# Letting the last group's three table stores leave together, with a GpSimd drain behind each unit's gathers

## The chip, the cores and the metric

The kernel runs on one core of one Trainium2 chip. The metric is the device time of one execution in microseconds (us). A core has five engines that run side by side: TensorE (PE, with its weight loads as PEld), VectorE (DVE), ScalarE (ACT), GpSimd (POOL) and SyncE (SP). SP issues most transfers; POOL issues those whose rows are picked by an index tile. One transfer is carried by the core's DMA engines and reports its end through a semaphore.

## The reference

Three stages follow one another: a pooled attention, a dense two-layer block, and a mixture of experts in which each token goes to the one expert with the largest logit.

```python
x = attention(q, k, v)                       # 2304 tokens of 512
h = x @ w_in; g = where(h >= 1, h, where(h <= -1, 0, (h + 1)**2 / 4)); x = g @ w_out
logits = normalise(x) @ normalise(expert_emb).T / tau
e = argmax(logits); gate = softmax(logits)[e]
out[token] = gate * (relu(x[token] @ w1[e]) @ w2[e])      # 8 experts, d_ff 1024
```

## The kernel before, in words

Attention runs over pairs of heads, the dense block over four groups of token tiles (five, five, five and three tiles of 128 tokens). The rows of each finished group are written to `y_rows` in DRAM, and the `Router` works out, per group, each token's expert, its gate, and its place in a table in DRAM (`self.tab`). An entry of the table is four words: the row of `y_rows`, the row of the output, the gate, and nothing. Each expert has its own stretch of the table. The entries of one tile are written by one indirect store that POOL issues (`scatter`, L924 to L927): index column `i` of `pu` says where the 128 entries of tile `i` go. For the first three groups these stores are put into a list and issued later, two per step; for the last group they follow at once, in a loop (L928 to L932).

The expert stage (`Moe2`) goes through units of 256 table entries of one expert. For unit `u`, `gather` (L1180) lets SP read the first table row of the unit from the small tile `units` (L1181), load the unit's 256 entries (`records`, L1186) into a tile `d_rec`, and lets POOL fetch the token rows these entries name by two indirect gathers (`rows`, L1191) into tiles `d_xg`. TensorE transposes them (`x_t`, `x_tile`, L1198), ACT and DVE split them into a high and a low part (L1202, L1203), and `hidden` (L1219) and `outer` (L1255) are the two layers. POOL stores the results by output row (`store`, L1263). All engines run the order in which the code is written; POOL's order is therefore: the last group's three table stores, the two gathers of unit 1, the store of unit 0's first half, the store of its second half, the gathers of unit 2, and from then on for each unit its stores and then the gathers of the unit after next. A unit with at most 128 tokens takes the shorter `half` path (L1224) and has one store.

Unit 0 is special. Its expert is known early, from the first three groups, and its work (`hidden` and `outer` in `run`, L1337 to L1367) runs while the last group is still being routed. Unit 1 is the first that needs the table complete. Between the end of the last group's logits and unit 1 the chain is: DVE computes `pu` (L922), POOL issues the three stores one by one, each behind the landing of the one before, because all three write the tile `self.tab`; DVE meanwhile works out the units (`units`, L1026, its result at L1072); SP reads `units` and loads `d_rec`; POOL gathers; TensorE transposes. On SP the loads of unit 1's weights stand behind the load of `d_rec`; the weights are the same as unit 0's here, so that these loads are skipped by their condition.

The tiles `d_rec` are a ring of three, `d_xg` and `d_ob` (outputs and the shorter path's intermediates) rings of four, so an engine that falls behind holds up the others only when a ring is used up.

Of the kernel before, what the change touches and what calls it, by code (L numbers as in the profile page):

```python
# [8 lines left out]
F32 = mybir.dt.float32  # L9
# [18 lines left out]
UNIT = 256  # L28
# [662 lines left out]
class Router:  # L691
# [9 lines left out]
    def consts(self, stage):  # L701
        nc, t, g = self.nc, self.one.tile, self.nc.gpsimd
        kw = dict(allow_small_or_imprecise_dtypes=True)
        self.iota = t([128, E], F32, name="iota_e")
        g.iota(self.iota, pattern=[[1, E]], base=-E, channel_multiplier=0, **kw)
        self.base = t([128, E], F32, name="base_e")
        g.iota(self.base, pattern=[[N, E]], base=0, channel_multiplier=0, **kw)
        self.iu = t([1, UMAX + 1], F32, name="iota_u")
        g.iota(self.iu, pattern=[[1, UMAX + 1]], base=0, channel_multiplier=0, **kw)
        yield  # L710
        self.two = t([1, UMAX + 1], F32, name="powers")
        g.memset(self.two[:, 0:1], 1.0)
        a = 1
        while a <= UMAX:
            m = min(a, UMAX + 1 - a)
            g.tensor_scalar(out=self.two[:, a:a + m], in0=self.two[:, 0:m], scalar1=2.0 ** a, scalar2=1.0,
                            op0=ALU.mult, op1=ALU.mult)
            a += m
        yield
        self.acc = t([128, E], BF16, name="acc")  # L720
        g.memset(self.acc, 0.0)

        self.ids = t([128, 18, 4], U32, name="ids")
        g.memset(self.ids.bitcast(F32), 0.0)
        ids = self.ids.bitcast(I32)
        g.iota(ids[:, 0:15, 0], pattern=[[128, 15]], base=0, channel_multiplier=1)
        g.iota(ids[:, 15:18, 0], pattern=[[128, 3]], base=ZROW + 1, channel_multiplier=1)
        yield
        for p0, n, tile0 in ((0, 4, 0), (4, 1, 16), (5, 12, 4), (17, 1, 17)):
            if n > 1:  # L730
                g.iota(ids[:, p0:p0 + n, 1], pattern=[[NQ, n // 4], [128, 4]], base=tile0 // 4 * NQ,
                       channel_multiplier=1)
                continue
            for h in range(2):
                p = slice(h * 64, h * 64 + 64)
                g.iota(ids[p, p0:p0 + 1, 1], pattern=[[0, 1]], base=(2 * (tile0 - 16) + h) * NQ + 512,
                       channel_multiplier=1)
        yield

        n = E * N // 128  # L740
        rows = stage.tile([128, 1024], I32, name="m", tag="m")[:, 0:4 * n]
        for c, v in enumerate((ZROW, 4095, 0, 0)):
            g.iota(rows.rearrange("p (r c) -> p r c", c=4)[:, :, c], pattern=[[0, n]], base=v, channel_multiplier=0)
        nc.sync.dma_start(out=self.tab.rearrange("(p r) c -> p (r c)", p=128), in_=rows.bitcast(U32))
        nc.sync.dma_start(out=self.y[ZROW:ZROW + 1, :].rearrange("a (p c) -> (a p) c", p=8), in_=self.cn["zero"][0:8])
        yield
        ones, upper = (stage.tile([128, 512], F32, name="w", tag="w")[:, 0:128] for _ in range(2))
        g.memset(ones, 1.0)
        g.affine_select(out=upper, in_=ones, pattern=[[1, 128]], compare_op=ALU.is_gt, fill=0.0,
                        base=0, channel_multiplier=-1)  # L750
        self.ones = t([128, 128], BF16, name="ones_b")
        g.tensor_copy(self.ones, ones)
        self.upper = t([128, 128], BF16, name="upper_b")
        g.tensor_copy(self.upper, upper)
        self.tau = t([128, 1], F32, name="tau")
        nc.sync.dma_start(out=self.tau, in_=self.tau_in.to_broadcast([128, 1]))
# [34 lines left out]
    def group(self, g, yps, m1, m2):  # L791

        nc = self.nc
# [25 lines left out]
        def small(name, dt=F32):  # L819
            return sm.tile([128, 5, E], dt, name=name)[:, :nt]  # L820

        def one(name, dt=F32):
            return sm.tile([128, 5], dt, name=name)[:, :nt]
# [15 lines left out]
        def transpose(i):  # L839
            def f():  # L840
                if last and i < 2:
                    p = m2.pt()
                else:
                    p = (spare[i % 2] if spare else bank("yt_ps")).rearrange("p (k t) -> p k t", k=4)
                for k in range(4):
                    nc.tensor.transpose(p[:, k], ys[i][:, k * 128:(k + 1) * 128], self.cn["idf"])
                yt = d["yt", i] = yts()

                def ev():
                    if i % 2:  # L850
                        nc.vector.tensor_copy(yt, p)
                    else:
                        nc.scalar.copy(yt, p)
                    if not last:
                        square(i)
                return ev() if last else ev
            return f
# [53 lines left out]
        def ev():  # L911
            ids = self.ids[:, p0:p0 + nt]
            p = d["p"]
            r, pf, pu = small("rk"), one("pf"), one("pu", U32)
            nc.vector.tensor_tensor(out=r, in0=p[:, 0:nt * E].rearrange("p (t e) -> p t e", e=E),
                                    in1=self.base[:, None, :].to_broadcast(sh), op=ALU.add)
            nc.vector.tensor_reduce(out=d["s"], in_=d["ex"], axis=AX.X, op=ALU.add)
            nc.vector.tensor_tensor(out=r, in0=r, in1=d["oh"], op=ALU.mult)
            nc.vector.tensor_scalar_add(d["s"], d["s"], 1e-9)
            nc.vector.tensor_reduce(out=pf, in_=r, axis=AX.X, op=ALU.add)  # L920
            nc.vector.reciprocal(ids[:, :, 2].bitcast(F32), d["s"])
            nc.vector.tensor_copy(pu, pf)  # L922

            def scatter(i):  # L924
                nc.gpsimd.indirect_dma_start(
                    out=self.tab, out_offset=bass.IndirectOffsetOnAxis(ap=pu[:, i:i + 1], axis=0),
                    in_=ids[:, i, :], in_offset=None)  # L927
            for i in range(nt):  # L928
                if last:
                    scatter(i)  # L930
                else:
                    m1.scat.append(lambda i=i: scatter(i))  # L932
            if not last and not spare:
                for i in range(nt):
                    nc.vector.tensor_add(self.acc, self.acc, d["oh"][:, i])
# [39 lines left out]
        out = []  # L975
        if spare:
            def both(i):
                def f():
                    t = transpose(i + 1)() if i + 1 < nt else lambda: None
                    e = logits(i)()  # L980
                    return lambda: (t(), e())
                return f
            out = [transpose(nd)] + [both(i) for i in range(nd, nt)]
# [120 lines left out]
class Moe2:  # L1104
# [74 lines left out]

    def gather(self, u):  # L1180
        row = self.nc.sync.value_load(self.rt.u[0:1, u, 0:1], min_val=0, max_val=E * N - UNIT)  # L1181
        rec = self.records(row, self.rec())
        return rec, self.rows(rec, [self.xg() for _ in range(2)])

    def records(self, row, rec):
        self.nc.sync.dma_start(out=rec, in_=self.rt.tab[bass.ds(row, UNIT), :].rearrange("(t p) c -> p t c", p=128))  # L1186
        return rec

    def rows(self, rec, xs, n=N + 1):
# [315 lines left out]
```

## Time and profile before

| | |
|---|---|
| time, median of 3 runs | 1203.81 us (1201.74 to 1203.91) |
| the profiled execution's own time | 1205.57 us |
| its span, first to last instruction | 1203.8 us |
| mean granted TensorE clock | 0.983 of full speed |
| busy: PE, DVE, ACT, POOL | 1149.5, 883.3, 740.3, 600.7 us |

The span is what the rows below are counted in, from its start; 1.77 us of the profiled execution's time lie around it. The expert stage begins at about 917 us of the span, and from about 956 us unit 1 runs. A row of a timeline gives the start, the time taken, the engine, the line, what is written from what, the number of instructions, and in brackets the idle time of the engine before it and what ended it. Rows that are merged give the time from the first start to the last end.

### The profile page before, as it was taken

The page shows a single profiled execution, that of the slowest core. Times are in us where ns is not written, and L with a number is a line of the kernel's source. Part 1 is how long each engine was busy: PE and PEld are TensorE (multiplying, and loading weights), DVE is VectorE, ACT ScalarE, POOL GpSimd, SP SyncE. Part 2 cuts the span into 40 slices and gives each one's busy share as a digit, 9 for nine tenths or more (in the row PEclk, how much of TensorE's full clock was granted, in tenths as well). Part 3 has the DMA queues.
Part 4 walks back from the last instruction along what each step waited for, and adds up shares of the span by engine and source line. Part 5 has one row for each costly group of instructions (what it writes and reads, how often), then busy time and mean ns, then how long its engine had stood idle before and what let it go on. Part 6 is the DMA issues. An engine that isn't in the chain of part 4 may idle for free. (4 is left out here: it accounts for less than half of the span.)

```text
span 1203.8 us, 21165 instructions
## 1 busy us (share of the span) xinstructions
PE 1149.5 (95%) x7315; PEld 1068.2 (89%) x7315; DVE 883.3 (73%) x1593; ACT 740.3 (61%) x1451; POOL 600.7 (50%) x523
## 2 busy tenths in 40 slices
PE   7999999999999999799789999999999899999995
PEld 7999999999999999688679889988989798888794
DVE  6888988999999998698745664664444767576663
ACT  5888888878788787343335444444445466576663
POOL 7998988777888883699930230013020311122121
PEclk9999999999999999999899999999999899999998
DMA  7787777785868753564332212111240111376533
GB/s 187 179 184 179 165 186 171 171 209 126 205 162 205 173 137 103 158 194 147 101 106 65 66 45 76 56 34 31 97 159 27 40 51 38 116 256 191 177 106 110
DMA packets 87189, 156.14 MB, mean 130 GB/s; under 512 B 26871, under 2 KB 44279, under 8 KB 87056
## 3 DMA queue, kind: packets, MB, share of 16 engines
q1 hardware_dynamic: 82352, 142.34, 44.2%
q0 software_dynamic: 4336, 11.58, 2.9%
q8 instruction: 67, 1.10, 0.4%
q10 hardware_dynamic: 368, 0.59, 0.2%
q14 instruction: 66, 0.54, 0.2%
HBM read 145.84 MB, written 20.08 MB: 138 GB/s over the span
## 5 line engine op out<-in xcount | busy, mean ns | idle before, releaser
L235 DVE TENSOR_SCALAR_CACHE_REDUCE e<-sc 128x1152 f32<-128x1152 f32 x144 | 194.7, 1352 | 25.0 <-PE sc L231 23.8
L242 ACT ACTIVATE e<-e,nm 128x1152 f32<-128x1152 f32 x144 | 183.7, 1276 | 4.4 <-DVE e L235 4.4
L231 PE MATMUL sc<-kT,qt 128*128 128x384 f32 x780 | 159.8, 340 | 9.2 <-DVE e L235 7.5
L269 ACT CAST pth<-pa 128x768 fp32r<-128x768 f32 (+2 forms) x160 | 116.3, 737 | 83.4 <-PE pa L260 83.4
L271 DVE TENSOR_TENSOR ptl<-pa,pth 128x768 fp32r<-128x768 f32 (+2 forms) x160 | 138.8, 876 | 20.6 <-ACT pth L269 8.4
L1166 DVE TENSOR_TENSOR e<-e,e 128x512 fp32r<-128x512 f32 x200 | 129.4, 686 | 33.0 <-ACT e L1165 16.4
L582 DVE SCALAR_TENSOR_TENSOR u<-h,u 128x320 f32<-128x320 f32 (+1 forms) x112 | 55.7, 497 | 124.8 <-ACT u L581 124.7
L578 ACT ACTIVATE u<-h,half 128x320 f32<-128x320 f32 (+1 forms) x112 | 59.7, 533 | 139.1 <-PE h L563 125.6
L231 PEld LDWEIGHTS sc<-kT,qt 128*128 128x128 f32 x780 | 132.8, 189 | 11.5 <-DVE e L235 9.1
L1255 PE MATMUL d_po<-e,e 128*128 128x512 f32 x504 | 122.6, 396 | 0.5 <-DVE e L1166 0.5
L260 PE MATMUL pa<-idf,e 128*128 128x128 f32 x864 | 118.2, 273 | 1.7 <-DVE ptl L271 1.7
L1165 ACT CAST e<-e 128x512 fp32r<-128x512 f32 x200 | 113.7, 619 | 4.6 <-DMA e<-moe_w 4.1
L595 PE MATMUL y<-wh,gl 128*128 128x512 f32 x288 | 114.0, 396 | 0.5 <-POOL gl L586 0.5
L595 PE MATMUL y<-wh,gh 128*128 128x512 f32 x288 | 114.0, 396 | 0.0
L595 PE MATMUL y<-wl,gh 128*128 128x512 f32 x288 | 113.6, 395 | 0.0
L1263 POOL DMA_INDIRECT out<-d_ob,d_rec x19 | 21.9, 1154 | 181.1 <-ACT d_ob L1262 150.7
L1255 PEld LDWEIGHTS d_po<-e,e 128*128 128x128 f32 x504 | 93.5, 190 | 19.4 <-DVE e L1166 0.9
L260 PEld LDWEIGHTS pa<-idf,e 128*128 128x128 f32 x864 | 103.4, 141 | 7.1 <-DVE ptl L271 1.3
L584 ACT CAST gh<-u 128x320 fp32r<-128x320 f32 (+1 forms) x112 | 52.4, 468 | 87.3 <-DVE u L582 87.3
L563 PE MATMUL h<-xth,wh 128*128 128x320 f32 (+1 forms) x448 | 89.8, 322 | 16.6 <-POOL wh L57 9.8
L285 PE MATMUL av<-pth,vh 128*128 128x288 f32 x576 | 103.5, 307 | 0.0
L535 POOL TENSOR_TENSOR xl<-xth,xl 128x512 f32<-128x512 f32 (+1 forms) x14 | 18.4, 1311 | 168.4 <-DMA xl<-av_t 86.6
(256 smaller groups left out, 2644.6 us busy)
## 6 DMA issues: line engine op xcount, KB each, us to landing
e<-moe_w SPq DMA_DIRECT2D x104, 512.0 KB
kr<-k SPq DMA_DIRECT2D x63, 288.0 KB
qr<-q SPq DMA_DIRECT2D x62, 288.0 KB
kk<-kT SPq DMA_DIRECT2D x60, 288.0 KB
vr<-v SPq DMA_DIRECT2D x16, 576.0 KB
av_b<-avs SPq DMA_DIRECT2D x64, 128.0 KB
wi<-moe_w_in SPq DMA_DIRECT2D x16, 512.0 KB
wo<-moe_w_out SPq DMA_DIRECT2D x16, 512.0 KB
```

Of the source, the lines that this page charges most:

```text
L231: nc.tensor.matmul(s[:, j, 0:384], lhsT=a, rhs=b[:, 384 * j:384 * j + 384], start=i == 0, stop=i == len(mm) - 1)
L235: nc.vector.tensor_scalar(out=e.rearrange("p (a b) -> p a b", a=3), in0=s[:, :, 0:384], scalar1=-0.5 / D ** 0.5, scalar2=None, op0=ALU.mul ...
L242: self.nc.scalar.activation(e, e, AF.Exp, bias=d["nm"][:, t:t + 1], scale=-1.0, accum_out=d["sum"][:, t:t + 1])
L260: nc.tensor.transpose(p[:, c // 3, (c % 3) * 128:(c % 3) * 128 + 128], e[:, i * 128:(i + 1) * 128], idf)
L269: nc.scalar.copy(hi, p)
L271: nc.vector.tensor_sub(out=lo, in0=p, in1=hi.bitcast(F32))
L285: nc.tensor.matmul(box["t"][:, 0:GQ], lhsT=self.vh[:, h * 9 + i % 9], rhs=p[:, i % 9, c0:c0 + GQ], start=i == 0, stop=i == 17)
L563: nc.tensor.matmul(ps[:, :n], lhsT=a[:, k], rhs=b[:, k, h0:h0 + n], start=i == 0, stop=i == 11)
L595: self.nc.tensor.matmul(y, lhsT=a, rhs=b, start=j == 0 and q == 0, stop=j == NF - 1 and q == 2)
L1165: self.nc.scalar.copy(hi, r)
L1166: self.nc.vector.tensor_sub(out=lo, in0=r, in1=hi.bitcast(F32))
L1255: self.nc.tensor.matmul(self.o, lhsT=(self.hh, self.hl)[a][f // 4][:, f % 4, s], rhs=self.w[b, f // 2][:, f % 2], start=f == 0 and q == 0, ...
```

## The change

The three stores of the last group are declared not to depend on one another. Between two of them stands a memset of one float of a new tile, `between`. The load of the table's entries for unit 1 is given a dependence on each of the three stores (before, it waited on the last of them, which had waited on the others). And `gather` ends with a drain of GpSimd behind its two gathers, once in each unit from unit 1 on, which no engine waits for by a semaphore; the instructions behind it on POOL come after it.

```diff
+        self.between = t([1, 4], F32, name="between")
...
             def scatter(i):
-                nc.gpsimd.indirect_dma_start(
+                return nc.gpsimd.indirect_dma_start(
                     out=self.tab, out_offset=bass.IndirectOffsetOnAxis(ap=pu[:, i:i + 1], axis=0),
-                    in_=ids[:, i, :], in_offset=None)
+                    in_=ids[:, i, :], in_offset=None).ins
+            done = self.scattered = []
             for i in range(nt):
                 if last:
-                    scatter(i)
+                    if i:
+                        nc.gpsimd.memset(self.between[:, i:i + 1], 0.0)
+                    inst = scatter(i)
+                    for other in done:
+                        self.tc.declare_no_dep(inst, other, reason="each token has a row of its own")
+                    done.append(inst)
...
     def gather(self, u):
         row = self.nc.sync.value_load(self.rt.u[0:1, u, 0:1], min_val=0, max_val=E * N - UNIT)
-        rec = self.records(row, self.rec())
-        return rec, self.rows(rec, [self.xg() for _ in range(2)])
-
-    def records(self, row, rec):
-        self.nc.sync.dma_start(out=rec, in_=self.rt.tab[bass.ds(row, UNIT), :].rearrange("(t p) c -> p t c", p=128))
+        rec = self.records(row, self.rec(), self.rt.scattered if u == 1 else ())
+        xs = self.rows(rec, [self.xg() for _ in range(2)])
+        self.nc.gpsimd.drain()
+        return rec, xs
+
+    def records(self, row, rec, after=()):
+        inst = self.nc.sync.dma_start(out=rec, in_=self.rt.tab[bass.ds(row, UNIT), :]
+                                      .rearrange("(t p) c -> p t c", p=128)).ins
+        for a in after:
+            self.tc.add_manual_dep(inst, a.name, mybir.DependencyInfo(mybir.DependencyClass.Sync,
+                                                                      mybir.DependencyReason.DATA),
+                                   reason="reads the rows that each of them writes")
         return rec
```

POOL's order before, from the last group's first table store to unit 0's first output store, with what each instruction waits for (DMASW are the landings of POOL's own transfers, DMAHW those of SP's, the others engines; drains are not listed in these orders):

```order
476 L925 DMA table<-ids,pu 18432x4 [waits DMASW6_49,DVE_49]
477 L925 DMA table<-ids,pu 18432x4 [waits DMASW1_49]
478 L925 DMA table<-ids,pu 18432x4 [waits DMASW2_49]
479 L1191 DMA d_xg_10603<-y_rows,d_rec_10597 128x512 [waits DMAHW5_49,DMAHW4_49,DMAHW6_49,DMAHW3_49,PE_49]
480 L1191 DMA d_xg_10600<-y_rows,d_rec_10597 128x512 [waits PE_49]
481 L1263 DMA out<-d_ob_10604,rec_10331 2304x512 [waits Activation_49]
```

The same stretch of POOL with the change (the line numbers are those of the changed kernel):

```order
476 L926 DMA table<-ids,pu 18432x4 [waits DMASW6_49,DVE_49]
477 L933 MEMSET between 1x1
478 L926 DMA table<-ids,pu 18432x4
479 L933 MEMSET between 1x1
480 L926 DMA table<-ids,pu 18432x4
481 L1205 DMA d_xg_10604<-y_rows,d_rec_10598 128x512 [waits DMAHW5_49,DMAHW4_49,DMAHW6_49,DMAHW3_49,PE_49]
482 L1205 DMA d_xg_10601<-y_rows,d_rec_10598 128x512 [waits PE_49]
483 L1277 DMA out<-d_ob_10605,rec_10332 2304x512 [waits Activation_49]
```

The second and third store have lost their waits (DMASW1 and DMASW2), and a memset stands ahead of each. On SP the load of unit 1's entries stood before as

```order
695 L1181 TENSOR_LOAD units [waits DVE_49]
696 L1181 ISA x2
697 L1186 ISA
698 L1186 DMA d_rec_10597<-table 128x2x4 [waits DMAHW6_49,DMASW3_49,PE_49]
699 L1286 TENSOR_LOAD units
```

and stands now as

```order
695 L1188 TENSOR_LOAD units [waits DVE_49]
696 L1188 ISA x2
697 L1195 ISA
698 L1195 DMA d_rec_10598<-table 128x2x4 [waits DMASW3_49,DMASW2_49,DMAHW6_49,DMASW1_49,PE_49]
699 L1300 TENSOR_LOAD units
```

so that the two waits that POOL no longer makes have moved to SP. No instruction has changed its place on SP, PE, ACT or DVE.

## Rows read from the trace of the kernel before

**Rows 1.** The page, part 1: busy time, share of the span and instructions of each engine.

```profile
PE 1149.5 (95%) x7315; PEld 1068.2 (89%) x7315; DVE 883.3 (73%) x1593; ACT 740.3 (61%) x1451; POOL 600.7 (50%) x523
```

**Rows 2.** Timeline of PE (start, us taken) around the first transposes of unit 1.

```profile
941.88 5.52 PE L1255 MATMUL d_po<-e,e 128*128 128x512 f32 x23 [0.52 <-DVE e L1166]
952.03 1.11 PE L1198 MATMUL d_pt<-idf,d_xg 128*128 128x128 f32 x4 [4.63 <-DMA d_xg<-y_rows,d_rec]
...
957.06 0.64 PE L1219 MATMUL d_ph<-d_xl,e 128*128 128x256 f32 x4
```

**Rows 3.** Timeline of POOL, from the last group's table stores to unit 0's outputs.

```profile
934.11 1.05 POOL L925 DMA_INDIRECT table<-ids,pu  x1 [4.91 <-DVE u_nu L1036]
937.10 1.95 POOL L925 DMA_INDIRECT table<-ids,pu  x1 [1.94 <-DMA table<-ids,pu]
941.96 1.30 POOL L925 DMA_INDIRECT table<-ids,pu  x1 [2.91 <-DMA table<-ids,pu]
948.65 0.98 POOL L1191 DMA_INDIRECT d_xg<-y_rows,d_rec  x1 [5.39 <-DMA d_rec<-table]
949.94 0.97 POOL L1191 DMA_INDIRECT d_xg<-y_rows,d_rec  x1 [0.30 <-issue]
951.21 1.03 POOL L1263 DMA_INDIRECT out<-d_ob,rec  x1 [0.31 <-issue]
959.29 1.09 POOL L1263 DMA_INDIRECT out<-d_ob,rec  x1 [7.05 <-ACT e L1221]
```

**Rows 4.** SP between 930 and 990 us: its waits (total, times, longest), and its timeline.

```profile
SPq L1186 <- DMA table<-ids,pu: 4.1, 1, 4.1
...
946.13 0.40 SPq L1186 DMA_DIRECT2D d_rec<-table  x1
```

**Rows 5.** Timeline of DVE: the instruction that completes the tile `units`.

```profile
941.05 0.18 DVE L1072 CAST units<-u_res 1x54 int32<-1x54 f32 x1
```

**Rows 6.** All 18 table stores (ns min/median/max), and POOL's waits for their landings.

```profile
L925 POOL DMA_INDIRECT table<-ids,pu x18: 957/964/1947, 715.4 to 942.0; - x18
...
POOL table L925 <- DMA table<-ids,pu: 30.6, 14, 4.5
```

**Rows 7.** Groups of POOL: a memset of one element (busy us, mean ns, idle before).

```profile
L712 POOL MEMSET powers<- 1x1 f32 x1 | 0.1, 89 | 0.0
```

**Rows 8.** Windows (PE, PEld, DVE, ACT, POOL busy; granted PE clock; DMA share, GB/s).

```profile
950.00:950.25 0.25, 0.00 (x0) 0.00 (x0) 0.25 (x2) 0.25 (x1) 0.25 (x1) 0.57 0.00 0
...
957.00:958.00 1.00, 1.00 (x10) 1.00 (x10) 1.00 (x2) 1.00 (x3) 0.00 (x0) 1.00 0.00 0
...
1051.70:1054.00 2.30, 2.30 (x7) 1.88 (x8) 1.82 (x4) 0.79 (x2) 0.27 (x1) 0.66 0.13 36
...
1091.50:1095.00 3.50, 3.50 (x15) 2.87 (x16) 2.37 (x4) 1.73 (x4) 0.23 (x1) 1.00 0.42 132
```

**Rows 9.** Timeline of PE in later units.

```profile
967.95 0.86 PE L1255 MATMUL d_po<-e,e 128*128 128x512 f32 x3
968.65 1.03 PE L1198 MATMUL d_pt<-idf,d_xg 128*128 128x128 f32 x8
...
1051.70 1.42 PE L1233 MATMUL d_ph<-e,d_xh 128*128 128x512 f32 x4 [2.22 <-ACT e L1165]
...
1091.49 1.17 PE L1233 MATMUL d_ph<-e,d_xh 128*128 128x512 f32 x4 [1.66 <-ACT e L1165]
```

**Rows 10.** Timeline of ACT and DVE: the split of unit 1's second tile.

```profile
955.32 0.59 ACT L1202 CAST d_xh<-d_pt 128x512 fp32r<-128x512 f32 x1 [1.55 <-PE d_pt L1198]
955.94 0.69 DVE L1203 TENSOR_TENSOR d_xl<-d_pt,d_xh 128x512 fp32r<-128x512 f32 x1 [1.44 <-ACT d_xh L1202]
```

**Rows 11.** Landing times of lines L1191 and L1263; timeline of POOL, its tightest store.

```profile
DMA to landing us min/median/max: 3.3/4.8/6.7
...
DMA to landing us min/median/max: 3.1/7.9/8.5
...
1106.64 1.02 POOL L1263 DMA_INDIRECT out<-d_ob,d_rec  x1 [8.08 <-ACT d_ob L1262]
```

## The prediction

> **What bounds the kernel now.** I read the page first, then the waits of TensorE, and from there the chain backwards through POOL and SP. TensorE is busy for 95% of the span [rows 1], so time can be won only where it stands still or runs slowly. The largest hole in the expert stage, and the one that this change can reach, lies ahead of unit 1: TensorE ends unit 0's last ready work at 947.40 us and starts unit 1's first transposes at 952.03 us, 4.63 us later, and the trace names the gather of the token rows as what ended the wait [rows 2].
>
> Backwards from there: the gather starts at 948.65 us, behind the load of the table entries [rows 3]; SP issued that load at 946.13 us, after 4.1 us of waiting for the table stores to land, so SP had reached it at 942.0 us [rows 4]. The stores themselves run one behind another: the second starts 1.94 us after the first has been issued, the third 2.91 us after the second, and the third's own landing comes 946.13 - 943.26 = 2.87 us after its issue ends [rows 3, 4]. So three landings stand in a row, and two of them are there only because of the order between the stores.
>
> The hole costs more than its length. While TensorE stood still its granted clock fell from full speed (2.4 GHz) to half (1.2 GHz), in the quarter of a microsecond after 950.00 us, that is 2.6 us after its last matmul; it is back at full speed in the window from 957 us [rows 8]. Four transposes take 1.11 us there, where eight take 1.03 us at full clock [rows 2, 9]. The stretch from 952.03 to 957.06 us therefore belongs to the price of the hole.
>
> **The change, part by part.**
>
> *The two landing waits go.* Store 1 still starts at 934.11 us and ends at 935.16 us. Behind it come a gap, a memset, a gap and the next store. A one-element memset took 0.089 us with no idle ahead of it [rows 7]; two transfers that POOL issues without a wait stand 0.30 us apart [rows 3]. Memset and gaps thus lie between 0.1 and 0.7 us; I take 0.5. A store takes 0.96 to 1.95 us [rows 6]; here 1.05, 1.95 and 1.30 [rows 3], and I take the middle one, 1.30. Store 2 then runs from 935.66 to 936.96 us, store 3 from 937.46 to 938.76 us, and with 2.9 us of landing (the second and third store's, against 1.94 for the first) the table is complete at 941.65 us. The ends: with 0.1, 0.96 and 1.94 us it is 939.2 us; with 0.7, 1.95 and the longest landing wait of the trace, 4.5 us [rows 6], it is 945.0 us.
>
> The store at 937.10 us, with 1.95 us twice as long as the median of 0.964 [rows 3, 6], runs beside DVE's subtractions. The Trainium skill (GPSIMD Engine Reference, section 8) says that GpSimd shares its SBUF interfaces with VectorE and contends with its instructions of two SBUF inputs, of which the weight splits are one; it speaks against packing the stores into DVE's busiest stretch. By that rule both moved stores would take 1.95 us, the table would be complete at 942.95 us, and the sum below would be smaller by 0.75 us. The first store met the same splits and took 1.05 us, so the trace agrees only in part, and I stay at 1.30.
>
> *What is late next on SP.* The load of the entries cannot go before 942.0 us in any case, because SP reads `units` first, which DVE completes at 941.23 us [rows 5]. SP now also waits on two more semaphores; I allow 0.2 us. The load goes at 942.2 instead of 946.13 us: **3.9 us earlier**. SP's weight loads behind it, which are skipped, and the splits of ACT and DVE that wait for them move by the same amount; both engines have room there.
>
> *The gathers.* Load to gather took 948.65 - 946.13 = 2.52 us and gather to transposes 3.38 us [rows 2 to 4]. The first transposes then start at 942.2 + 2.52 + 3.38 = 948.1 us. TensorE's hole shrinks from 4.63 to 0.7 us.
>
> *The clock.* An idle of 1.66 us ahead of 1091.49 us left the clock at 1.00, one of 2.22 us ahead of 1051.70 us brought it down (0.66 over the next 2.3 us) [rows 8, 9]. A hole of 0.7 us should leave it at full speed. Then from 948.13 us: four transposes and three matmuls take 0.5 + 0.7 us (half of the eight, and the step from 967.95 to 968.65 us [rows 9]) and end at 949.3; the second gather, 1.29 us behind the first, lands at 949.42 at the same 3.38 us; its transposes are out 0.6 us later, at 950.05; ACT's copy takes 0.59 and DVE's subtraction 0.69 with small gaps, as now [rows 10], to 951.4 us. The low part's matmuls, now at 957.06 us [rows 2], start at 951.45 us. That is **5.6 us earlier**: 3.9 us of the hole and 1.7 us of the slow stretch, which is bounded by 0 (clock falls as now) and 2.5 us (everything in 5.03 us at double speed, no data waited for). From there the units run as before, since loads, splits and stores of later units all hang on the units ahead of them.
>
> *The drains.* The trace shows no drain. From below it costs nothing that shows; from above, it holds POOL until everything POOL has issued has landed, which is at most 6.7 us from the issue of a gather and 8.5 us from that of an output store [rows 11]. Take the upper end. In unit 1 the store that now follows at 951.21 us [rows 3] would go at 949.5 us, when the second gather has landed, instead of 947.3; its output tile is one of four, the next store needs it landed (3.1 us at best) only at 959.29 - 5.6 = 953.7 us, and nobody waits. In later units the next store stands idle for at least 8.08 us for its data [rows 11], while the gathers have landed 5.7 us after their issue ended (6.7 less 0.97), and an output store ahead of them 8.5 - 3.6 = 4.9 us after it. The cover is 8.08 us, and 2.4 us of it is left. Cost: 0. If the cover went, a late store would first delay the next unit's gathers, and then the transposes.
>
> **Sum:** 3.9 + 1.7 + 0 = 5.6 us. The profiled execution took 1205.57 us and becomes 1200.0 us; the median of the runs, 1203.81 us, lies 1.76 us lower, and I carry the difference over: **1198.2 us**.
>
> **The rivals.**
>
> *The clock stays low.* The hole is short but follows another of 0.52 us [rows 2] and is followed by a third while the second gather lands. If these together bring the clock down, only 3.9 us are won: 1199.9 us. For it speaks that the matmuls between the holes are few; against it the idle of 1.66 us at full clock [rows 9]. 0.20.
>
> *The three landings get in each other's way.* A store landed 4.5 us after its issue elsewhere [rows 6]. With the upper ends above, the table is complete at 945.0 us, 1.1 us are won on SP, the hole remains 3.5 us, the clock falls as now: 1202.7 us. Against it: three stores of 128 entries of 16 bytes are little data. 0.12.
>
> *The change does not do what it says.* If POOL holds each memset until the store ahead of it has landed, the old waits of 1.94 and 2.91 us remain and the memsets with their gaps come on top, 2 x 0.4 us: 1204.6 us. The order shows the waits gone, so this would have to be a habit of the engine. 0.07.
>
> *Slower: the memset brings a pause of its own.* It stands between the stores, and POOL has run no memset since the early setup. A pause p at each puts the table's completion at 941.65 + 2p, and from p = 2.2 us on this is later than now. With p = 4.5 us, the longest wait POOL has had behind a table store [rows 6], SP's load goes at 950.7 us, 4.5 us later than now: 1208.3 us. Against it: the memset of one element in the setup had no idle ahead of it, though other kinds of instruction preceded it [rows 7]. 0.05.
> The Trainium skill (GPSIMD Engine Reference, section 2.1) says that the first call of a freshly loaded kernel on GpSimd costs about 6 us with no instruction to be seen; if that struck both memsets, an estimate from the page would be 7.5 us lost. No run here shows it.
>
> **How the numbers follow.** My forecast has 0.56. A change of 0.2% (2.4 us) is about what a measurement of this kernel can tell from none. Forecast and low clock give faster: 0.76; half-way cases of the late landing (between 2.4 and 3 us won) add 0.02. Same: the rest of the late landing, 0.10, and the change that does nothing, 0.07, 0.17 in all. Slower: 0.05. The range: the forecast's own bounds reach from 2.5 instead of 1.7 us for the clock (1197.4) to the rule's 0.75 us (1199.0); the runs before spread over 2.2 us, so I go 1 us lower, to 1196.4, and up to 1202.2 us, which takes in the low clock with the slower stores (3.1 us won, 1200.7 us) and the better half of the late landing. Outside are left the useless change, the pause, and the worse half of the late landing: 0.18.
>
> **What would show it.** In the profile after: three table stores within 5 us from 934.1 us, with idle of about 0.3 us and a memset between them; SP's wait at the load of the entries gone or below 1 us, the load near 942 us; the idle ahead of the first transposes of unit 1 below 1 us; granted clock 1.00 from 945 to 960 us; the first `hidden` of unit 1 5 to 6 us earlier, and every later unit by the same. A TensorE hole over 2 us, a clock of 0.50 behind it, POOL busy or held at the output stores past the end of ACT's scaling, or later gathers landing behind TensorE by more than now would each prove a step wrong.

## The result, and the profile after

The changed kernel takes 1191.05 us (median of 4 runs, 1190.73 to 1192.92) against 1203.86 us for the kernel before, a ratio of 0.9892 with a 95% interval of 0.9876 to 0.9908: 12.8 us faster, where 5.6 us were forecast and 1196.4 us was the low end of the range. The profiled execution took 1190.95 us, with a span of 1189.1 us against 1203.8 us; the two spans differ by 14.7 us, 1.9 us more than the medians do.

The part of the span that the prediction worked out came as it was worked out. The page's busy line, answering to [rows 1]:

```profile
PE 1145.3 (96%) x7315; PEld 1064.7 (90%) x7315; DVE 882.1 (74%) x1593; ACT 740.6 (62%) x1451; POOL 600.4 (50%) x525
```

POOL's timeline around the table stores, to be laid beside [rows 3]; and the next instructions that hung on it, on SP and DVE [rows 4, 5]:

```profile
933.63 1.05 POOL L926 DMA_INDIRECT table<-ids,pu  x1 [4.17 <-DVE u_nu L1043]
934.69 0.09 POOL L933 MEMSET between<- 1x1 f32 x1
934.99 0.97 POOL L926 DMA_INDIRECT table<-ids,pu  x1 [0.21 <-issue]
935.97 0.09 POOL L933 MEMSET between<- 1x1 f32 x1
936.27 0.96 POOL L926 DMA_INDIRECT table<-ids,pu  x1 [0.21 <-issue]
944.23 0.98 POOL L1205 DMA_INDIRECT d_xg<-y_rows,d_rec  x1 [7.00 <-DMA d_rec<-table]
945.51 0.97 POOL L1205 DMA_INDIRECT d_xg<-y_rows,d_rec  x1 [0.30 <-issue]
950.81 1.03 POOL L1277 DMA_INDIRECT out<-d_ob,rec  x1 [4.33 <-ACT d_xh L1216]
...
941.70 0.40 SPq L1195 DMA_DIRECT2D d_rec<-table  x1
...
940.59 0.18 DVE L1079 CAST units<-u_res 1x54 int32<-1x54 f32 x1
```

The three stores leave within 2.64 us instead of 7.85, the memsets take 0.09 us, and the load of the entries follows 0.93 us behind the end of the instruction that completes `units`. Counted from the first table store, so that what happened earlier in the execution drops out, the load went at 12.02 us before and goes at 8.07 us now. TensorE's timeline, beside [rows 2]:

```profile
937.03 9.94 PE L1269 MATMUL d_po<-e,e 128*128 128x512 f32 x42
947.66 0.66 PE L1212 MATMUL d_pt<-idf,d_xg 128*128 128x128 f32 x4 [0.70 <-DMA d_xg<-y_rows,d_rec]
...
951.12 0.74 PE L1233 MATMUL d_ph<-d_xl,e 128*128 128x256 f32 x4
```

The window around the first matmul behind the hole (length, busy time of each engine, clock and DMA share, columns as in [rows 8]):

```profile
947.70:949.00 1.30, 1.30 (x7) 0.84 (x7) 0.51 (x2) 0.59 (x1) 0.00 (x0) 1.00 0.34 132
```

The hole is 0.70 us, the clock stays at 1.00, and the first low-part matmul of unit 1 comes 17.49 us behind the first table store instead of 22.95: 5.46 us.

What the prediction left out lies at the other end. Before, the last output store starts at 1192.22 us and the span ends at 1203.8 us, 11.58 us later; now it starts at 1184.14 and the span ends at 1189.1 us, 4.96 us later:

```profile
1192.22 1.00 POOL L1263 DMA_INDIRECT out<-d_ob,d_rec  x1 [4.21 <-ACT d_ob L1262]
...
1184.14 1.00 POOL L1277 DMA_INDIRECT out<-d_ob,d_rec  x1 [4.19 <-ACT d_ob L1276]
```

The instructions of the program's last line, the program's end, in the kernel before (ns min/median/max, first and last start), with the step of POOL ahead of them that counts a store which a branch leaves out (INC_SWDGE_SEM, here the counting step):

```profile
L1501 POOLq DRAIN  x3: 46/103/5468, 1197.5 to 1203.5; - x3
L1501 SPq DRAIN  x3: 7/7/13, 1197.7 to 1203.2; - x3
L1501 DVEq DRAIN  x2: 10/14/17, 1190.2 to 1203.2; - x2
...
L1297 POOLq INC_SWDGE_SEM  x1: 1470/1470/1470, 1195.6 to 1195.6; - x1
```

The same in the changed kernel, and the drains that the change adds (line 1191):

```profile
L1515 POOLq DRAIN  x3: 46/103/212, 1187.7 to 1188.9; - x3
...
L1311 POOLq INC_SWDGE_SEM  x1: 217/217/217, 1187.3 to 1187.3; - x1
...
L1191 POOLq DRAIN  x12: 5067/6177/8604, 944.5 to 1164.7; - x12
```

POOL's drain at the end took 5.47 us and takes 0.21; the counting step took 1.47 us and takes 0.22. Together that is 6.5 of the 6.62 us. The span's 14.7 us are thus 0.48 us from ahead of the first table store (933.63 against 934.11 us, stages that the change does not touch), 5.46 us up to unit 1, 2.14 us between unit 1 and the last output store, and 6.62 us at the end.

### The profile page after: what moved, and what is told of

Its sections match the earlier page's. It is cut to its first block, busy times and chain, and to the rows that moved or that the text cites. A ratio compares the mean times of both kernels' runs of the same rounds, so it can differ in the third digit from the quotient of the medians.

```text
span 1189.1 us, 21181 instructions
## 1 busy us (share of the span) xinstructions
PE 1145.3 (96%) x7315; PEld 1064.7 (90%) x7315; DVE 882.1 (74%) x1593; ACT 740.6 (62%) x1451; POOL 600.4 (50%) x525
## 3 DMA queue, kind: packets, MB, share of 16 engines
q0 software_dynamic: 4336, 11.58, 2.9%
```

## The experiments

Two theories stood for the end. A: the last drain retires what POOL has issued since the drain before it, so its length goes with the number of those transfers; before, 65 transfers (18 table stores, 26 gathers, 21 output stores) in 5.47 us, 0.084 us each. B: the end is short because what the last drain waits for had more time to land.

**The stores alone.** The changed kernel without the drain:

```diff
         xs = self.rows(rec, [self.xg() for _ in range(2)])
-        self.nc.gpsimd.drain()
         return rec, xs
```

> The three table stores leave together as in the changed kernel, with no drain in any unit. Theory A (the drain that ends the program has to retire every transfer that POOL issued since the last drain, about 5.47/65 = 0.084 us each): the final drain is 5.4 to 5.5 us again, the step that counts a store not made at the end is 1.0 to 1.5 us, the end lies 11 to 12 us behind the start of the last store, and the time is 1191.05 + 6.6 = 1197.6 us. Theory B (the end is short because the stages ahead of it are earlier, so that what the final drain waits for has landed): the end stays at 5 us behind the last store and the time at 1191 us.

1199.88 us (5 runs) against 1204.64 us of the kernel before, run beside it (11 runs), a ratio of 0.9959 (0.9944 to 0.9975). In its trace the final drain and the counting step:

```profile
L1514 POOLq DRAIN  x3: 46/103/5460, 1193.2 to 1199.2; - x3
...
L1310 POOLq INC_SWDGE_SEM  x1: 1460/1460/1460, 1191.3 to 1191.3; - x1
```

The end is 11.56 us long again, although unit 1 and all behind it are as early as in the changed kernel (the load of the entries 8.06 us, the first low-part matmul 17.35 us behind the first table store). Theory B falls. The total is 2.3 us above what theory A gave (1197.6 us).

**The drains alone.** The kernel before, with the drain:

```diff
         rec = self.records(row, self.rec())
-        return rec, self.rows(rec, [self.xg() for _ in range(2)])
+        xs = self.rows(rec, [self.xg() for _ in range(2)])
+        self.nc.gpsimd.drain()
+        return rec, xs
```

> The table stores wait for one another as before; only the drain behind each unit's gathers is added. Theory A: the final drain takes 0.2 us, the time is 1203.86 - 6.6 = 1197.3 us, the hole ahead of unit 1 is 4.6 us and TensorE's clock falls to 0.50 in it. Theory B: no gain, 1203.9 us. If the drains cost something in the units, the gain is smaller than 6.6 us and the output stores of the short units start later than ACT has their data.

1199.28 us (6 runs), ratio 0.9948 (0.9930 to 0.9966). The last drain takes 0.212 us and the end 5.11 us; ahead of unit 1 the old hole is there, and the slow matmuls behind it:

```profile
L1503 POOLq DRAIN  x3: 50/103/212, 1198.4 to 1199.5; - x3
...
952.72 1.11 PE L1200 MATMUL d_pt<-idf,d_xg 128*128 128x128 f32 x4 [4.61 <-DMA d_xg<-y_rows,d_rec]
953.48 1.63 PE L1257 MATMUL d_po<-e,e 128*128 128x512 f32 x3
...
957.88 0.64 PE L1221 MATMUL d_ph<-d_xl,e 128*128 128x256 f32 x4
```

The load of the entries goes 12.03 us behind the first table store and the low-part matmul 23.06 us, as before. The total is 2.0 us above what A gave, as that of the stores alone is 2.3 us above. So each part does its own work. The two gains, 4.8 and 5.4 us, add up to 10.1 us where the whole change gave 12.8; the product of the two ratios is 0.9907, inside the interval of the whole change (0.9876 to 0.9908), near its end, so that what is missing cannot be told from scatter.

**One drain, early.** The changed kernel, drained once, behind unit 1's gathers:

```diff
-        self.nc.gpsimd.drain()
+        if u == 1:
+            self.nc.gpsimd.drain()
```

> The changed kernel with a single drain, behind unit 1's gathers. Theory A: 22 gathers and 21 output stores are left to the final drain, 43 x 0.084 = 3.6 us, and the counting step at the end is 0.8 to 1.0 us; the time is 1191.05 + 3.4 + 0.7 = 1195.2 us. Theory B, or a drain that matters only once: 1191 us; if a drain has to stand in every unit to help at all, 1197.6 us.

1195.03 us (6 runs), ratio 0.9932 (0.9914 to 0.9949). Its final drain, the counting steps of the three short units and that of the end:

```profile
L1516 POOLq DRAIN  x3: 52/103/3655, 1186.8 to 1191.0; - x3
...
L1321 POOLq INC_SWDGE_SEM  x3: 589/705/845, 1058.7 to 1136.3; - x3
...
L1312 POOLq INC_SWDGE_SEM  x1: 1020/1020/1020, 1185.3 to 1185.3; - x1
```

3.655 us for the 43 transfers that were left, where A gave 3.6. From 65 to 43 transfers the drain loses 1.81 us, 0.082 us each. The bytes do not set it: 18 of these 22 are table stores of 128 entries of 16 bytes, while the 43 others move token rows of 512 floats, and from 43 to 2 transfers the drain loses 0.084 us each. All of them are transfers of 128 rows, so the number of rows and the number of transfers are not told apart.

**One drain, late.** The same with `if u >= 12`, so that only the last gathers that run are drained.

> The changed kernel with a single drain, behind the last gathers that run (unit 12's, issued in unit 11). Theory A: this one drain takes the landing and some 63 x 0.084 = 5.3 us, about 9 to 11 us in all, inside the 11.6 us that POOL waits there for the next store's data; the final drain is 0.2 us and the time 1191 us, up to 1 us more for the counting steps of the short units (1.0 to 1.2 us instead of 0.2). If the earlier eleven drains matter for another reason, the time is nearer to 1197.6 us.

1191.42 us (4 runs), ratio 0.9890 (0.9872 to 0.9909), the changed kernel's time with one drain instead of twelve:

```profile
L1192 POOLq DRAIN  x1: 9871/9871/9871, 1165.7 to 1165.7; - x1
...
L1516 POOLq DRAIN  x3: 46/103/320, 1188.4 to 1189.3; - x3
...
L1321 POOLq INC_SWDGE_SEM  x3: 1029/1145/1285, 1059.1 to 1137.8; - x3
```

and POOL's first store behind that drain, in its timeline:

```profile
1179.46 1.21 POOL L1278 DMA_INDIRECT out<-d_ob,d_rec  x1 [11.34 <-ACT d_ob L1277]
```

The retiring has not gone away: this drain ends at 1175.6 us, and POOL's next store has its data at about 1179 us. It lies where POOL waits anyway, and the end is 4.65 us long. The counting steps of the short units are as long as before. What they may cost is less than these totals can show, whose intervals are about 2 us to either side.

**More memsets.** The changed kernel with six memsets ahead of the second and the third store:

```diff
-                        nc.gpsimd.memset(self.between[:, i:i + 1], 0.0)
+                        for _ in range(6):
+                            nc.gpsimd.memset(self.between[:, i:i + 1], 0.0)
```

> The changed kernel with six memsets instead of one ahead of the second and of the third table store. If SP's load waits for the tile of units and not for the stores (the third store's landing at about 940.1 us against 941.6 us), the second and third stores start 0.5 to 1 us later each and the load of the entries stays 8.07 us behind the first store. If the stores set it, the load moves by 1 to 2 us. If a memset brings a pause of its own, it shows as idle ahead of a memset.

1190.19 us (one run). The timeline of POOL, and SP's load:

```profile
933.46 1.05 POOL L926 DMA_INDIRECT table<-ids,pu  x1 [3.92 <-DVE u_nu L1044]
934.52 0.82 POOL L934 MEMSET between<- 1x1 f32 x6
935.50 0.97 POOL L926 DMA_INDIRECT table<-ids,pu  x1 [0.16 <-issue]
936.47 0.82 POOL L934 MEMSET between<- 1x1 f32 x6
937.45 0.96 POOL L926 DMA_INDIRECT table<-ids,pu  x1 [0.16 <-issue]
...
941.50 0.40 SPq L1196 DMA_DIRECT2D d_rec<-table  x1
```

The third store starts 3.99 us behind the first instead of 2.64, and the load still goes 8.04 us behind it. What is late next on SP is the tile `units`, with at least 1.35 us to spare for the stores; and no memset brings a pause. No run left the memsets out, so whether the stores need them is not shown.

**Output stores that do not wait for one another.** In the changed kernel POOL still waits for landed output stores (42.0 us in 5 waits), and the gathers of the next unit stand behind. Two kernels take that order away as the change did for the table, one with all drains and one with the late drain alone:

```diff
-        nc.gpsimd.indirect_dma_start(out=self.out,
+        inst = nc.gpsimd.indirect_dma_start(out=self.out,
...
-                                     in_=o, in_offset=None, bounds_check=N - 1, oob_is_err=False)
+                                            in_=o, in_offset=None, bounds_check=N - 1, oob_is_err=False).ins
+        for other in self.outs:
+            self.tc.declare_no_dep(inst, other, reason="each token has a row of its own")
+        self.outs.append(inst)
```

> The changed kernel, and in addition the output stores of the units are declared not to depend on one another, so that the second store of a unit goes when ACT has its data and not when the first has landed. The waits of 7.2 to 9.0 us of POOL for a landed output store go; ahead of the short units the gathers start some 2 to 3 us earlier and TensorE's waits for them (2.5 us in the changed kernel) go or halve: 1189 to 1190 us. If POOL's drains then set when the stores go, or the gathers were early enough, it is the same as the changed kernel, 1191 us.

> The same with a single drain, behind the last gathers that run. The final drain stays at 0.2 to 0.4 us, the counting steps of the short units are 1.0 to 1.3 us, and POOL is not held in the units before. If holding POOL in each unit costs something, this is faster than the run with all drains by up to 1 us (1188.5 to 1190 us); if the counting steps cost more than the drains do, it is slower by about 1 us.

Beside them ran the changed kernel again:

> The changed kernel again, beside the others of this call: 1191 us by the first measurement, and the same distances in its trace as there: first table store to the load of the entries 8.07 us, to unit 1's first low-part matmul 17.4 us, last output store to the end 5.0 us.

1189.53 us (0.9886, interval 0.9858 to 0.9915), 1189.97 us (0.9888, 0.9864 to 0.9911), and 1192.11 us for the changed kernel (0.9898, 0.9865 to 0.9930), 6 runs each. The intervals overlap. The kernel with the late drain alone (counting steps of 1.04 to 1.29 us, final drain 0.308 us) is neither faster nor slower than the one with all drains by more than that. The first and the last were run once more:

> The changed kernel with independent output stores, again, beside the changed kernel itself: 1189.5 us by the first measurement, 1.5 to 2.5 us below the changed kernel in the same call. In its trace unit 1's first low-part matmul to the last output store takes 230 us (233 us in the changed kernel) and TensorE waits about 0.9 us for gathers. If the first measurement was scatter, the two are equal and the stretch is 232 to 234 us in both.

> The changed kernel a third time: 1191 to 1192 us, 233 us from unit 1's first low-part matmul to the last output store, 2.5 us of TensorE's waits for gathers, final drain 0.2 us.

1191.50 us (0.9891, 0.9864 to 0.9917) and 1191.72 us (0.9885, 0.9862 to 0.9907): the same. From unit 1's first low-part matmul to the last output store the kernel with free output stores took 233.4 us, where 230 was expected, and the changed kernel 232.8 us. TensorE's waits from 930 us on (total, times, longest), and its stretch from unit 1's first low-part matmul to the last output store (columns as in [rows 8]), show where the gain went. In the kernel with free output stores:

```profile
PE d_ph L1248 <- ACT e L1173: 4.6, 2, 2.4
PE d_ph L1248 <- issue: 1.0, 1, 1.0
PE d_pt L1213 <- DMA d_xg<-y_rows,d_rec: 0.7, 1, 0.7
...
951.50:1184.80 233.30, 226.59 (x1404) 201.82 (x1404) 159.76 (x272) 149.20 (x298) 46.60 (x42) 0.99 0.42 137
```

In the changed kernel beside it:

```profile
PE d_pt L1212 <- DMA d_xg<-y_rows,d_rec: 5.0, 6, 1.1
PE d_ph L1247 <- ACT e L1172: 2.6, 1, 2.6
PE d_ph L1247 <- ACT d_ob L1276: 1.3, 1, 1.3
...
952.30:1185.00 232.70, 224.19 (x1404) 199.19 (x1404) 160.07 (x272) 149.51 (x298) 45.75 (x42) 1.00 0.43 137
```

The waits for gathers went, from 5.0 us (2.5 had been expected) to 0.7 us, while those for the split weights of the short units rose by 2.0 us. In all TensorE stands idle for 6.7 us of the stretch instead of 8.5, but the same 1404 matmuls take 2.4 us longer, at a mean granted clock of 0.99 instead of 1.00, and this takes the gain away. In the first profiles of the two kernels with free output stores TensorE is idle for 5.4 and 5.9 us of the stretch, and in every kernel whose output stores wait for 7.0 to 8.5 us; the times of whole runs do not tell them apart. No version was shown to beat the change. The distances that were expected of the repeated kernel came within 0.6 us (8.13 us to the load, 17.97 us to the low-part matmul, 5.2 us at the end).

## Why the prediction was wrong

*The landing waits: right.* 3.9 us were forecast for SP's load; it is 12.02 - 8.07 = 3.95 us. The cost between two stores was taken as 0.5 us and is 0.30 us, and a store as 1.30 us and takes 0.97; neither matters, since `units` sets the load (the run with more memsets shows it): the instruction that completes `units` ends 0.93 us ahead of the load, where the prediction had allowed 0.97.

*The rule on SBUF interfaces.* As the prediction read it, both moved stores would have taken 1.95 us. They took 0.97 and 0.96 us here, and the kernel in which only the drains were added still has one store of 2.09 us at the old place. DVE's weight splits beside the stores, two by two, before and in the changed kernel:

```profile
936.92 1.27 DVE L1166 TENSOR_TENSOR e<-e,e 128x512 fp32r<-128x512 f32 x2
941.15 1.28 DVE L1166 TENSOR_TENSOR e<-e,e 128x512 fp32r<-128x512 f32 x2
...
933.75 1.27 DVE L1173 TENSOR_TENSOR e<-e,e 128x512 fp32r<-128x512 f32 x2
936.46 1.28 DVE L1173 TENSOR_TENSOR e<-e,e 128x512 fp32r<-128x512 f32 x2
```

Before, the store of 1.95 us starts at 937.10 us, while a pair of splits runs, and ends 0.86 us behind the pair; the one of 1.30 us ends 0.83 us behind the next pair. In the changed kernel the second store starts 0.03 us ahead of a pair's end, the third 0.19 us ahead of a pair's start. Over all twelve traces each of the last group's stores that starts inside a pair ends 0.83 to 0.95 us behind it, and the others take 0.96 to 1.06 us, even where a pair starts within them. So the traces agree with the rule of the Trainium skill (GPSIMD Engine Reference, section 8), and the first store, which the prediction held against it, had started 0.12 us ahead of its pair; at the new places the rule did not cost anything. No run moved the stores against the splits to test this.

*The hole and the clock: right.* A hole of 0.7 us was forecast, and it is 0.70; the clock stayed at 1.00; 5.6 us to the low-part matmul were forecast and 5.46 measured, 3.95 and 1.5 us where 3.9 and 1.7 had been added up. In all ten traces without the landing waits that distance is 17.35 to 18.08 us; in the two with them 22.95 and 23.06 us. In the ten the granted clock is 1.00 over the 4.5 us from the first transposes on, so the rival in which the clock stays low is refuted there.

*The drains: wrong.* The step that failed is the sentence "The trace shows no drain" with the cost of 0 that follows from it. The trace of before does show drains, on the program's last line, and one of POOL with 5.47 us; I read the expert stage to its last output store and took the 11.58 us behind that as given. So the sum lacks a term of 6.5 us: 5.26 us of drain and 1.25 us of counting step, which the end no longer has because the added drains take that time earlier, inside POOL's idle. The added drain was weighed as a cost alone, between nothing and a held store; no rival had it win time, and all that was left outside the range was slower. What was said of their price in the units held: twelve drains of 5.07 to 8.60 us each. The first held the store of unit 0's first half, and with it, by its landing, the second half's store, which starts 3.24 us behind unit 1's first low-part matmul where it starts at 2.6 us in the kernels with neither that drain nor the hole; the next output store is at 18.1 us in both. Each of the other eleven ended at least 3.5 us ahead of POOL's next output store (one of 7.2 us from 1126.6 us, say, at 1133.8 against 1137.31 us). The Trainium skill (VectorE: DVE Perf Modes, section "The DRAIN you can't avoid") says that the drains of a program's beginning and end take about 12 ns on all five engines; SP and DVE agree with 7 to 17 ns, POOL with 5468 ns does not, if the drains of this program's last line are among those it means.

*The total.* Stores alone give 1199.88 us, 4.8 us less than the kernel before, run beside it, where 5.6 us less was forecast for everything; drains alone give 5.4 us.

*Open.* The 2.14 us between unit 1's first low-part matmul and the last output store. 0.63 us lie ahead of unit 4's first output store: 87.40 us behind that matmul in most kernels without the hole (87.8 in two), 88.03 in both with it. The rest, from there to the last output store, with the short units in it, takes 144.6 to 148.8 us in the kernels whose output stores wait for each other, and does not follow the place of the drains (145.62 and 148.78 us with drains in every unit, 147.06 without any). TensorE over the whole stretch, before and in the changed kernel:

```profile
957.10:1192.20 235.10, 227.46 (x1406) 201.87 (x1404) 159.76 (x272) 149.02 (x297) 43.92 (x41) 0.99 0.42 135
...
951.10:1184.10 233.00, 225.85 (x1405) 200.89 (x1404) 159.88 (x272) 149.61 (x298) 46.94 (x42) 0.99 0.41 137
```

Of the difference 1.6 us is time of its matmuls and 0.5 us idle. Over the nine kernels whose output stores wait, the matmuls take 224.2 to 228.8 us and the idle is 7.0 to 8.5 us. From unit 4's first output store on, the same 820 matmuls take 136.5 to 137.0 us where the mean granted clock is 1.00 and 139.3 to 140.8 us where it is 0.98. So most of the scatter goes with the clock. The holes ahead of the short units lie near 2 us, and the clock fell in some of them and not in others: a hole of 2.22 us brought it down before [rows 8, 9] and left it at 1.00 in the profile after, where one of 2.06 us brought it down (0.67 from 1083.30 to 1086 us). What decides there was not found. Nor was it shown what the drain does for each transfer; only that its time goes with their number.

## What to carry to other kernels

Before costing an added instruction, look for the same instruction anywhere in the trace, the program's last microseconds included; the stretch behind the last store belongs to the time like any other. Where GpSimd has issued many transfers, the final drain is paid for each of them; one drain late in a wait that GpSimd has anyway (9.87 us here, done 3.9 us ahead of the next store) takes it off the end, and twelve showed no more. Stores that write different rows of one table need an order only against the reader, and what is then late next sets the gain: here the tile `units`, complete 0.93 us ahead of the load.

## What the runs showed of the hardware

A final drain on GpSimd took 5.468 and 5.460 us with 65 transfers issued since the drain ahead of it, 3.655 us with 43, and with 2 it took 0.212 us, or 0.308 and 0.320 us where a single late drain stood ahead; between 65, 43 and 2 that is 0.082 to 0.084 us for each. The step that counts a store not made (INC_SWDGE_SEM) grows with the same number, 1.03, 1.15, 1.29 and 1.47 us through the kernel before, and is 0.59, 0.71, 0.85 and 1.02 us with the first 22 transfers drained, 0.44 to 0.45 us less at each place; with a drain in every unit it is 0.17 to 0.22 us. A table store that GpSimd issued while a pair of DVE's weight splits ran ended 0.83 to 0.95 us behind the pair, in 14 of 14 cases; the other 22 took 0.96 to 1.06 us.
